# Where a diffusion block on one Trainium2 core waits for its earlier output stores: ahead of the issue of the last store, or behind it

## The chip, the cores and the metric

The kernel runs on one core of one Trainium2 chip. The metric is the device time of one execution in microseconds (us). One execution was also taken by the hardware profiler; its span runs from the first to the last profiled instruction, and positions such as "at 243.75" are microseconds from the start of that span. PE is the matmul engine, DVE the vector engine, ACT the scalar engine, POOL the GpSimd engine, and SP the engine that here does nothing but issue DMAs and wait on semaphores.

## What is computed

The reference is a transformer block with modulation, as diffusion models use it, for 2 batches of 256 tokens of width 1152, in bf16:

```python
mod = (silu(c) @ w_mod).reshape(B, 6, 1, D)
shift_a, scale_a, gate_a, shift_m, scale_m, gate_m = [mod[:, i] for i in range(6)]
h = layernorm(x) * (1 + scale_a) + shift_a
q, k, v = split(h @ wqkv)                 # 2 heads of 576
a = softmax(q @ k.T * Dh ** -0.5) @ v @ wo
x = x + gate_a * a
h2 = layernorm(x) * (1 + scale_m) + shift_m
m = gelu(h2 @ w_fc1) @ w_fc2              # 1152 -> 4608 -> 1152
return x + gate_m * m
```

Only the last line matters for the change: the product with `w_fc2`, the gate, the sum, and the store of the result.

## The kernel before, in words

**How the work is ordered.** The whole program is first written down as a list of small units, each for one engine, by helper functions (`dma` records its transfer at line 662, `mm` its matmul at line 681). `Sched.schedule` then plans them with estimated durations. For PE and SP the order is the order in which the units were written down; DVE and ACT take what is ready, the most urgent first. `Sched.emit` gives every instruction its waits and puts the instructions on the engines. A transfer that SP issues gets the next of 48 semaphores in turn, so the 14 output stores have one each, and no two of them share one. A DMA's semaphore is full, and the DMA "landed", when it has gone up by 16.

**The last stage** (lines 1131 to 1147). The 512 tokens are four tiles of 128 (`t`). Each tile's 1152 output columns are cut into pieces: three of 384 for tiles 0 to 2; 384, 384, 224, 96 and 64 for tile 3. A piece is 36 matmuls into one PSUM bank (line 1142), a DVE multiplication by the gate (line 1145), a DVE addition of the residual that writes the bf16 result (line 1146), and a store (line 1147, recorded at line 662) that SP issues when the addition is done. There are 14 pieces and so 14 stores, numbered here from 0: **store 11** is that of 224 columns (56 KB), **store 12** that of 96 columns (24 KB), **store 13**, the last, that of 64 columns (16 KB). In every one of them each of the 128 partitions writes one run of 448, 192 or 128 bytes for these three.

**The waits for stores.** The result buffers are three, used in turn, and DVE waits for the store that last used the buffer before it writes it again; those waits come from the planner and are not changed. Beside them SP itself waits for all stores, since the program must not end before they have landed. Where it does so is written by hand in `run_engine`, inside `emit`: `outs` is the list of the 14 stores in SP's order, `last_out` is store 13. Just ahead of `last_out` SP waits for `outs[:-2]`, stores 0 to 11 (lines 469 to 471), and then for the DVE addition of the last piece (line 476). Behind it SP waits for store 12 (lines 483 and 484) and for store 13 (line 485). In the program as it is built, SP has ahead of store 13 five instructions that each wait on two of the stores' semaphores (line 471), then one that waits on DVE and on store 1's semaphore (line 476); the wait for store 0 sits on the DMA instruction of store 13 itself. Behind it are one wait, for store 13 (line 485), and the branch that ends SP's part (line 554), which carries the wait for store 12. After it come SP's drain and the barrier of all engines.

Of the kernel before, what the change touches and what calls it, by code (L numbers as in the profile page):

```python
# [171 lines left out]
class Sched:  # L172
# [225 lines left out]
    def emit(self, nc, block, sems, dma_sems):  # L398
        order = self.order
        eidx = {e: 0 for e in ENGINES}  # L400
        dma_cnt = [0] * len(dma_sems)
        n_other = getattr(self, "n_other_dma_sems", 8)
        n_sp = len(dma_sems) - n_other
        di = 0
        dj = 0
        for e in ENGINES:
            for u in order[e]:
                for ins in u.instrs:
                    if u.dma_bytes > 0:
                        if e == "sp":  # L410
                            k = di % n_sp
                            di += 1
                        else:
                            k = n_sp + dj % n_other
                            dj += 1
                        dma_cnt[k] += 16
                        ins.dma_sem = k
                        ins.dma_val = dma_cnt[k]
                    else:
                        eidx[e] += 1  # L420
                        ins.eidx = eidx[e]
        self.final_counts = dict(eidx)
        self.final_dma = list(dma_cnt)
        snap = {}
        stats = {"waits": 0}

        def sem_of(d):
            if d.dma_sem is not None:
                return ("d", d.dma_sem), d.dma_val
            return ("e", d.unit.eng), d.eidx  # L430

        allu = sorted(self.units, key=lambda u: (u.start, u.uid))
        known = {e: {} for e in ENGINES}
        waits = {}
        for u in allu:
            e = u.eng
            kn = known[e]
            for ins in u.instrs:
                need = {}
                for d in ins.deps:  # L440
                    k, v = sem_of(d)
                    if need.get(k, 0) < v:
                        need[k] = v
                wl = []
                for k, v in sorted(need.items(), key=lambda kv: (-kv[1], str(kv[0]))):
                    if kn.get(k, 0) >= v:
                        continue
                    wl.append((k, v))
                    kn[k] = v
                    for d in ins.deps:  # L450
                        if sem_of(d) == (k, v):
                            sn = snap.get(d.gidx)
                            if sn:
                                for kk, vv in sn.items():
                                    if kn.get(kk, 0) < vv:
                                        kn[kk] = vv
                            break
                waits[ins.gidx] = wl
                stats["waits"] += len(wl)
                snap[ins.gidx] = dict(kn)  # L460
        self.wait_stats = stats

        outs = [ins for u in order["sp"] for ins in u.instrs if ins.is_out]
        last_out = outs[-1]

        def run_engine(e, eng_handle):
            for u in order[e]:
                for ins in u.instrs:
                    if ins is last_out:
                        for o in outs[:-2]:  # L470
                            eng_handle.wait_ge(dma_sems[o.dma_sem], o.dma_val)
                    for (k, v) in waits[ins.gidx]:
                        if k[0] == "d":
                            eng_handle.wait_ge(dma_sems[k[1]], v)
                        else:
                            eng_handle.wait_ge(sems[k[1]], v)
                    bi = ins.fn(eng_handle)
                    if ins.dma_sem is not None:
                        bi.then_inc(dma_sems[ins.dma_sem], 16)
                    else:  # L480
                        bi.then_inc(sems[e], 1)
            if e == "sp":
                for o in outs[-2:-1]:
                    eng_handle.wait_ge(dma_sems[o.dma_sem], o.dma_val)
                eng_handle.wait_ge(dma_sems[last_out.dma_sem], last_out.dma_val)

        block.sync(lambda eng: run_engine("sp", eng))
        block.tensor(lambda eng: run_engine("pe", eng))
        block.scalar(lambda eng: run_engine("act", eng))
        block.vector(lambda eng: run_engine("dve", eng))  # L490
        block.gpsimd(lambda eng: run_engine("pool", eng))
# [711 lines left out]
```

## Time and profile before

| | us |
|---|---|
| median of 3 runs | 248.95 (248.63 to 249.59) |
| the profiled execution's own time | 249.1 |
| its span, first to last instruction | 247.1 |
| PE busy in that span | 240.4 (97%) |
| mean granted clock of PE | 0.996 of full |
| last DVE instruction begins | 243.52 |
| store 13 is issued | 245.28 |
| last instruction begins | 247.08 |

The profiled execution's own time is 2.0 us more than its span, and 0.15 us above the median. The page has PE busy almost without a gap; its fifth part lists each group of instructions with the idle time of its engine before it, and its sixth the DMA issues with the median time from issue to landing. Beside the page, the trace answers for any stretch of time which instructions ran, what SP waited for, and how many DMA packets of each queue began in it. Queue q1 is the one on which SP's transfers run, 16 DMA engines in parallel; q8 and q14 carry instructions to the engines.

### The profile page before, as it was taken

To read this page: it belongs to the slowest core of one execution; us is meant where nothing else is said; L and a number is where in the kernel's file an instruction comes from. 1 tells how busy PE (TensorE), PEld (TensorE's weight loads), DVE (VectorE), ACT (ScalarE), POOL (GpSimd) and SP (SyncE) were. 2 spreads that over 40 slices of the span, in tenths; PEclk is the share of its full clock that TensorE was granted. 3 is DMA by queue.
4 is the path that set the end of the run, shared out by engine and by line. 5 is a ranking of instruction groups with operands and counts; after the bars stand their busy time and mean duration, and the time that the engine had idled before them with its cause. 6 is when DMAs were issued, how large, how long until landed. Compare 5 with 4: busy or idle time off the path is not lost.

```text
span 247.1 us, 4020 instructions
## 1 busy us (share of the span) xinstructions
PE 240.4 (97%) x1757; PEld 148.0 (60%) x1767; DVE 69.9 (28%) x179; ACT 64.0 (26%) x130; POOL 21.1 (9%) x35
## 2 busy tenths in 40 slices
PE   7999999999999999999999999999999999999993
PEld 2589844566656766798544444444666666666683
DVE  3742440546222779850000000000022111111122
ACT  5630340344312306983323332223000000000000
POOL 1300000000034175600000000000000000000000
PEclk9999999999999999999999999999999999999998
DMA  7999999999999999999953450000000000000000
GB/s 242 360 376 392 391 369 412 422 428 423 400 382 323 327 369 391 390 376 397 352 159 102 170 191 0 0 3 0 0 19 16 16 16 30 20 16 19 16 16 20
DMA packets 27708, 51.59 MB, mean 209 GB/s; under 512 B 1563, under 2 KB 15659, under 8 KB 26539
## 3 DMA queue, kind: packets, MB, share of 16 engines
q1 hardware_dynamic: 27216, 50.14, 56.1%
q0 software_dynamic: 448, 1.19, 1.5%
q8 instruction: 14, 0.23, 0.4%
q14 instruction: 3, 0.02, 0.0%
q10 hardware_dynamic: 27, 0.00, 0.0%
HBM read 50.14 MB, written 1.19 MB: 208 GB/s over the span
## 4 chain that ended last, share of the span: by engine, by line
PE 92%; DMA 3%; ACT 1%; SPq 1%; issue 0%; DVE 0%
PE psum L681 91%; DMA arena<-in_w_mod_dram 3%; PE psum L684 2%; ACT arena L1056 1%; SPq L662 1%; ACT arena L1040 1%; DVE arena L786 0%; DVE arena L1145 0%; DVE arena L1146 0%; DVE arena L777 0%
## 5 line engine op out<-in xcount | busy, mean ns | idle before, releaser
L681 PE MATMUL psum<-arena 128*128 128x384 bf16 (+8 forms) x1668 | 237.0, 312 | 2.4 <-POOL arena L704 1.4
L681 PEld LDWEIGHTS psum<-arena 128*128 128x128 bf16 (+1 forms) x1678 | 142.5, 97 | 92.2 <-issue 3.6
L1145 DVE TENSOR_TENSOR arena<-psum,arena 128x384 f32<-128x384 f32 (+3 forms) x14 | 7.0, 500 | 119.2 <-PE psum L681 119.2
L1066 ACT ACTIVATE arena<-psum 128x512 bf16<-128x512 f32 (+1 forms) x44 | 22.5, 522 | 42.6 <-PE psum L681 42.6
L676 ACT ACTIVATE arena<-psum 128x512 bf16<-128x512 f32 (+7 forms) x30 | 15.7, 546 | 35.7 <-PE psum L681 33.3
L678 DVE CAST arena<-psum 128x512 bf16<-128x512 f32 (+3 forms) x21 | 13.0, 627 | 26.4 <-PE psum L681 26.3
L1035 POOL TENSOR_TENSOR arena<-arena 128x384 f32<-128x384 f32 x12 | 10.9, 911 | 10.5 <-DVE arena L1034 9.3
L725 DVE BATCH_NORM_STATS2 arena<-arena 128x6 f32<-128x384 f32 (+1 forms) x18 | 9.5, 549 | 1.1 <-DMA arena<-in_x_dram 1.0
L1040 ACT ACTIVATE arena<-arena 128x1152 bf16<-128x1152 f32 x4 | 5.4, 1352 | 9.5 <-DVE arena L1039 9.5
L662 POOL DMA_DIRECT2D dit_scratch<-arena x4 | 2.7, 669 | 60.3 <-ACT arena L676 60.3
L684 PEld LDWEIGHTS psum<-arena 128*128 128x128 bf16 (+1 forms) x89 | 5.9, 98 | 2.7 <-DMA arena<-in_c_dram 0.8
L684 PE MATMUL psum<-arena 128*128 128x128 bf16 (+1 forms) x89 | 7.3, 219 | 0.2
L1034 DVE TENSOR_TENSOR arena<-psum,arena 128x384 f32<-128x384 f32 x12 | 6.6, 548 | 3.2 <-PE psum L681 2.6
L1146 DVE TENSOR_TENSOR arena<-arena 128x384 bf16<-128x384 f32 (+3 forms) x14 | 7.0, 501 | 0.5
L1056 ACT ACTIVATE arena<-psum,arena 128x128 bf16<-128x128 bf16 x16 | 6.1, 460 | 3.2 <-PE psum L684 2.5
L1053 DVE TENSOR_SCALAR arena<-psum,arena 128x128 bf16<-128x128 bf16 x20 | 5.5, 336 | 2.0 <-PE psum L684 1.8
L938 ACT ACTIVATE arena<-psum,arena 128x256 bf16<-128x256 f32 x8 | 3.7, 470 | 6.9 <-PE psum L681 5.4
L729 POOL TENSOR_TENSOR arena<-arena 128x1 f32<-128x1 f32 x6 | 3.3, 551 | 8.3 <-DVE arena L728 8.3
L901 ACT ACTIVATE arena<-arena 128x256 bf16<-128x256 bf16 x6 | 2.5, 495 | 3.3 <-DVE arena L895 3.3
L934 DVE TENSOR_REDUCE arena<-psum 128x2 f32<-128x512 f32 x4 | 2.8, 690 | 1.5 <-PE psum L681 1.5
L786 DVE TENSOR_SCALAR arena<-psum,arena 128x256 bf16<-128x256 bf16 x7 | 2.4, 349 | 2.7 <-PE psum L684 1.4
L942 DVE TENSOR_TENSOR arena<-arena 128x512 bf16<-128x512 bf16 x4 | 2.7, 687 | 0.1
(37 smaller groups left out, 32.0 us busy)
## 6 DMA issues: line engine op xcount, KB each, us to landing
arena<-in_w_mod_dram SPq DMA_DIRECT2D x3, 3456.0 KB, 26.5
arena<-in_w_fc_dram SPq DMA_DIRECT2D x9, 1152.0 KB, 8.8
arena<-in_w_fc_dram SPq DMA_DIRECT2D x4, 2592.0 KB, 20.9
arena<-in_wqkv_dram SPq DMA_DIRECT2D x18, 288.0 KB, 10.0
arena<-in_w_mod_dram SPq DMA_DIRECT2D x3, 864.0 KB, 12.5
arena<-in_wqkv_dram SPq DMA_DIRECT2D x1, 2592.0 KB, 10.9
arena<-in_wo_dram SPq DMA_DIRECT2D x1, 2592.0 KB, 39.0
arena<-in_w_mod_dram SPq DMA_DIRECT2D x3, 480.0 KB, 7.3
```

Source lines behind the costliest of these rows:

```text
L676: act(c_act(n), lambda e: e.activation(out=dst, in_=src, func=ACTF.Copy), [src], [dst], name)
L678: dve(c_dve_psum16(n) if psum16 else c_dve_psum32(n), lambda e: e.tensor_copy(dst, src), [src], [dst], name)
L681: S.instr(lambda e: e.matmul(o, lhsT=l, rhs=r, start=st, stop=sp, **kw), reads=[l, r], writes=[o])
L684: S.instr(lambda e: e.transpose(o, i_, idn), reads=[i_, idn], writes=[o])
L725: dve(550, lambda e, s=s, o=o: e.bn_stats(out=o, in_=s), [s], [o], "bn_%s_%d" % (tag, ci))
L1034: dve(550, lambda e, o=o, ga=ga, x1c=x1c: e.tensor_tensor(out=x1c, in0=o, in1=ga, op=ALU.mult), [o, ga], [x1c], "wo_t1_%d_%d" % (t, ci))
L1035: S.op("pool", 930, lambda e, xs=xs, x1c=x1c: e.tensor_tensor(out=x1c, in0=x1c, in1=xs, op=ALU.add), reads=[x1c, xs], writes=[x1c], name=" ...
L1040: act(1344, lambda e: e.activation(out=xn2, in_=x1, func=ACTF.Identity, scale=rs, bias=nm), [x1, rs, nm], [xn2], "xn2_%d" % t)
L1056: act(440, lambda e, o=o, dst=dst, s1=s1, s2=s2: e.activation(out=dst, in_=o, func=ACTF.Identity, scale=s1, bias=s2), [o, s1, s2], [dst], ...
L1066: act(c_act(ntok), lambda e: e.activation(out=dst, in_=o, func=ACTF.Gelu_apprx_tanh), [o], [dst], "gelu_%d_%d" % (f, tok0))
L1145: dve(c_dve_psum32(w), lambda e, o=o, gm=gm, t1=t1: e.tensor_tensor(out=t1, in0=o, in1=gm, op=ALU.mult), [o, gm], [t1], "fc2_t1_%d_%d" % ( ...
L1146: dve(c_dve_32(w), lambda e, t1=t1, x1c=x1c, ost=ost: e.tensor_tensor(out=ost, in0=t1, in1=x1c, op=ALU.add), [t1, x1c], [ost], "fc2_out_%d ...
```

## The change

SP no longer waits for stores 0 to 11 ahead of store 13. It issues store 13 as soon as the DVE addition of its piece is done, like every other store, and waits behind it for stores 0 to 12 and then for store 13.

```diff
             for u in order[e]:
                 for ins in u.instrs:
-                    if ins is last_out:
-                        for o in outs[:-2]:
-                            eng_handle.wait_ge(dma_sems[o.dma_sem], o.dma_val)
                     for (k, v) in waits[ins.gidx]:
...
             if e == "sp":
-                for o in outs[-2:-1]:
+                for o in outs[:-1]:
                     eng_handle.wait_ge(dma_sems[o.dma_sem], o.dma_val)
                 eng_handle.wait_ge(dma_sems[last_out.dma_sem], last_out.dma_val)
```

In the changed program as it is built, store 13's DMA instruction waits on DVE alone. Behind it stand seven wait instructions, the first on one semaphore and six on two (stores 7; 8 and 6; 9 and 5; 10 and 4; 11 and 3; 12 and 2; 13 and 1), and the closing branch carries the wait for store 0. SP has as many instructions as before, and the other engines have the same instructions in the same order. Three lines are gone from the file, so lines after 471 have numbers lower by three.

## The prediction

> **What bounds the kernel now.** I read the page first: its first part and its chain of waits.
>
> ```profile
> span 247.1 us, 4020 instructions
> PE 240.4 (97%) x1757; PEld 148.0 (60%) x1767; DVE 69.9 (28%) x179; ACT 64.0 (26%) x130; POOL 21.1 (9%) x35
> PE 92%; DMA 3%; ACT 1%; SPq 1%; issue 0%; DVE 0%
> ```
>
> PE sets the time up to its last matmul, and nothing that the diff touches is on PE. But that chain is followed back from the last DVE instruction, which ends at 243.75, and the span goes on to 247.1. The change can only act in these last 3.4 us, and there PE has nothing left to do. So I read that stretch by itself: its timeline, and then what SP waited for from 242 on (total, times, longest).
>
> ```profile
> 240.93 0.39 DVE L1146 TENSOR_TENSOR arena<-arena 128x224 bf16<-128x224 f32 x1
> 241.35 4.26 SPq L662 DMA_DIRECT2D out_dram<-arena  x3
> 242.32 0.26 DVE L1146 TENSOR_TENSOR arena<-arena 128x96 bf16<-128x96 f32 x1
> ...
> 243.52 0.23 DVE L1146 TENSOR_TENSOR arena<-arena 128x64 bf16<-128x64 f32 x1
> ```
>
> ```profile
> SPq L471 <- DMA out_dram<-arena: 1.9, 1, 1.9
> SPq L485 <- DMA out_dram<-arena: 1.1, 1, 1.1
> SPq L662 <- DVE arena L1146: 0.9, 1, 0.9
> ```
>
> The three last stores are issued from 241.35 on; the trace's records give 241.347, 242.610 and 245.279 for stores 11, 12 and 13. The last piece is done at 243.52 + 0.23 = 243.75, but its store goes out at 245.28: SP stands at line 471 for 1.9 us in one wait, and it is the fifth of the wait instructions there (from 243.2 to 245.15), the one that holds store 11. So the wait for a store of the piece before last is what holds the last store back.
>
> Why is store 11 late? The DMA view gives for any stretch the packets that began in it. First the issues with their times to landing (one row for stores 3 to 10, then 11, 12 and 13), then two stretches: 242.0 to 242.6 and 244.0 to 244.7.
>
> ```profile
> out_dram<-arena SPq DMA_DIRECT2D x8, 96.0 KB, 1.6
> ...
> out_dram<-arena SPq DMA_DIRECT2D x1, 56.0 KB, 3.8
> ...
> out_dram<-arena SPq DMA_DIRECT2D x1, 24.0 KB, 2.7
> ...
> out_dram<-arena SPq DMA_DIRECT2D x1, 16.0 KB, 1.4
> ```
>
> ```profile
> DMA packets 136, 0.07 MB, mean 117 GB/s; under 512 B 135, under 2 KB 135, under 8 KB 135
> ...
> q1 hardware_dynamic: 135, 0.05, 32.3%
> q8 instruction: 1, 0.02, 16.8%
> ```
>
> ```profile
> DMA packets 18, 0.01 MB, mean 7 GB/s; under 512 B 18, under 2 KB 18, under 8 KB 18
> ...
> q1 hardware_dynamic: 18, 0.01, 7.0%
> ```
>
> A store that meets nothing shows 144 packets on q1 (store 13 does, in 246.1 to 246.4): 128 rows and 16 small ones, nine on each of 16 DMA engines. Store 11 shows 135: one engine's nine are missing. In the same stretch one packet of 16 KB on q8, an instruction fetch, takes 16.8% of 16 engines over 0.6 us, which is 1.61 us of one engine, from 242.47 to 244.09. The missing nine, and nine of store 12, come right behind it: the 18 packets from 244.07 on. Store 11's semaphore has 15 of its 16 steps by 242.99 and the last at 245.14; store 12's by 244.10 and at 245.30. Store 8, issued at 226.53 and landed in 2.4 us instead of 1.6, met such a fetch too. So in this execution the waits ahead of store 13 do not pass for free: they wait for one DMA engine that is fetching instructions.
>
> **The change, part by part.**
>
> *The issue moves.* The two stores before it were issued 0.03 after their DVE addition (240.93 + 0.39 = 241.32 to 241.35; 242.32 + 0.26 = 242.58 to 242.61). Store 13 would go out at 243.75 + 0.03 = 243.78 instead of 245.28: **1.50 us earlier**. It issues one DMA and nothing else; no other queue is passed, since SP has nothing left to issue.
>
> *Its flight.* Store 13 took 245.279 to 246.693 = 1.41 us with no fetch beside it. From 243.78 the 15 free engines give 245.19. The engine that fetched is free at 244.09 and then has the 18 late packets until 244.67. Store 13's first packet began 0.83 after its issue, so at 243.78 + 0.83 = 244.61 in the changed kernel; its nine packets there come behind the 18. Two prices bound them. If they are as good as undisturbed, the store lands at 245.19 and store 12's 245.30 is the later. If the sixteenth engine's steps stay as far apart as those of stores 11 and 12 (245.14 to 245.30, 0.16), it lands at 245.30 + 0.16 = 245.46. Store 13's packets took 11 to 13 ns in this trace and store 12's on the late engine 20 to 49, so I take a point between, 245.40.
>
> [...]
>
> *The waits move behind.* Seven wait instructions and a branch now stand behind the issue, where one and a branch stood. SP's next instruction after issuing store 12 came 0.38 later (242.61 to 242.99), and waits that were already met followed each other every 0.06 to 0.07. So SP is at its first wait at 244.16 and past the fourth by 244.45, under the cover of the flight; without the cover the six added ones would cost 6 x 0.07 = 0.4. The fifth waits for store 11 until 245.15, the sixth for store 12 until 245.32, the seventh for store 13. If that has landed, SP is past it at 245.38, else 0.02 after the landing, at most 245.48. In the trace of before it is past this point at 246.71. The branch, the drain and the barrier behind it take 0.42 and stay: the branch then waits for store 0, landed long ago, as it now waits for store 12.
>
> *The sum.* 246.71 - 245.38 = 1.33 at best, 246.71 - 245.48 = 1.23 with the late engine; I take **1.25**. The span goes from 247.1 to 245.9, the profiled execution's 249.1 to 247.85. The median of the three runs is 0.15 below that execution, so the forecast is 248.95 - 1.25 = **247.7**.
>
> What is late next is store 11 itself, then 12, then 13, all on the engine that fetched: 0.1 us behind each other. The change takes the last store out of the queue behind the fetch, not the fetch out of the tail; the tail from 243.75 on would still hold 1.4 us of DMA and 0.4 of barrier.
>
> **The unknown.** The gain is as large as the stall, and the stall is as long as one fetch. The 14 fetches of 16 KB in the trace took 0.96 to 1.61 us, and the last is the longest. With 0.96 store 11 would land 0.65 earlier, at 244.48; store 13 of the kernel before would follow at 244.63 and land at 246.04, that of the changed kernel at 245.19 as before: gain 0.85. With no fetch in the way store 11 would have landed by 242.99, before the last piece is done, and only the wait instruction that carries DVE's semaphore goes, 0.07. A longer fetch raises both kernels and leaves 1.23. So the gain lies between 0.07 and 1.33.
>
> [...]
>
> **The rivals.**
> - *A shorter stall in the timed runs.* The profile is one execution, and its last fetch took 1.61 where the other 13 took 0.96 to 1.34. For it: that range. Against it: this fetch shares its engine with a store's packets at its start, and the profiled execution is only 0.15 slower than the median. Gain 0.85, **248.1**.
> - *No stall at all in the timed runs, or a landing that replaces it* (the last store takes its delay with it and lands after 246). Against it: most instructions that have to be fetched are PE's (3524 of the 4020), and those are the same in both. Gain under 0.1, **248.9**.
> - *Slower: the last store meets the fetch itself.* If the fetch began 1 to 2 us later in the changed kernel, store 13's share on that engine would be as late as store 11's was, 245.14 - 242.99 = 2.15 behind the other fifteen: 245.19 + 2.15 = 247.34 against 246.69, that is 0.65 slower, **249.6**. It decides from a fetch that ends after 245.6. Against it: PE reaches the same instruction at the same time, and no two of the trace's 16 KB fetches are closer than 9 us.
> - *That the change does not do what it says* can be left out: in the program as built, store 13 waits for DVE alone.
>
> **How the numbers follow.** Forecast 0.65, shorter stall 0.17, no stall 0.12, slower 0.06. The forecast's own range is 247.3 to 248.1 (1.23 to 1.33, and 0.3 for the median of a few runs, as the shown runs lie 0.3 below and 0.6 above theirs). The whole range takes in no stall, 248.9, and below 247.62 (1.33) the same scatter with some margin: 247.1 to 248.9. A change of 0.5%, about what a measurement of this kernel can tell from none, is 1.24 us; the forecast sits on that line. Of its 0.65 I put 0.48 beyond it; the rest, the shorter stall and no stall are within it. The slower case (0.65 us) is inside the line too, except with some scatter: 0.03.
>
> **What would show it.** Right: no wait at line 471's old place, store 13 issued at 243.8, 1.6 to 1.7 from issue to landing at most, store 11 still 3.8 and its wait now behind the issue, 18 or more late packets after the fetch, the span near 245.9. Wrong: a fetch in another place or of another length; store 13 needing over 2 us; or a tail of waits that goes on after the last landing by more than 0.1 above the present 0.42.

## The result, and the profile after

| | before | changed |
|---|---|---|
| median, first comparison | 249.0 us (6 runs, 248.1 to 249.59) | 247.55 us (6 runs, 247.18 to 248.06) |
| ratio, 95% interval | | 0.9947 [0.9924, 0.9971] |
| median, second comparison | 249.03 us (35 runs) | 248.01 us (12 runs) |
| ratio, 95% interval | | 0.9966 [0.9949, 0.9983] |
| span of the first profile | 247.1 us | 246.1 us |

The changed kernel is faster, by 1.45 us between the medians of the first comparison and by 1.02 in the second; the ratios, with their intervals, make it 0.7 to 1.9 us and 0.4 to 1.3. The forecast was 1.25 and a time of 247.7. These are the first two lines of the page of the changed kernel. PE has no more work than before: both programs have 1767 matmuls, of which the first trace lacks ten records.

```profile
span 246.1 us, 4030 instructions
PE 241.2 (98%) x1767; PEld 148.1 (60%) x1767; DVE 69.9 (28%) x179; ACT 64.0 (26%) x130; POOL 21.1 (9%) x35
```

Its timeline at the end, with line numbers lower by three than before:

```profile
241.54 3.02 SPq L659 DMA_DIRECT2D out_dram<-arena  x3
...
243.72 0.23 DVE L1143 TENSOR_TENSOR arena<-arena 128x64 bf16<-128x64 f32 x1
```

What SP waited for there (total, times, longest), and the three last stores from issue to landing:

```profile
SPq L659 <- DVE arena L1143: 4.5, 3, 2.8
SPq L481 <- DMA out_dram<-arena: 0.4, 1, 0.4
SPq L482 <- DMA out_dram<-arena: 0.2, 1, 0.2
```

```profile
out_dram<-arena SPq DMA_DIRECT2D x1, 56.0 KB, 3.7
out_dram<-arena SPq DMA_DIRECT2D x1, 24.0 KB, 2.6
out_dram<-arena SPq DMA_DIRECT2D x1, 16.0 KB, 1.7
```

The three issues now lie within 3.02 us instead of 4.26: store 13 follows its addition (243.72 + 0.23 = 243.94) at 243.97. SP's wait of 1.9 us for a store ahead of it is gone; 0.4 us of it is left behind the issue, at line 481. Store 11 is as late as before, 3.7 us. So what got faster is the moment at which the last store leaves.

The span holds a second thing that must be kept apart. The end of the last DVE addition came at 243.75 in the first profile of before and at 243.94 in that of the changed kernel; in a second profile of each, of the same programs, at 243.85 and 244.68. The part up to that addition thus differs by 0.1 us between the two executions of one program and by 0.7 between those of the other. All of this arises in the first 21 us: the second DVE instruction of line 777 (774 in the changed kernel, up to 779 in others) ends between 20.13 and 21.33 in the fourteen profiles of this study, and from there to the end of the last addition every one of them takes 223.36 to 223.41. I therefore read the **tail**, from the end of the last addition to the end of the span: 3.39 before, 2.16 changed. The difference, 1.23, is the change's gain in these two executions.

All kernels of this study, in us after the end of the last addition (negative: ahead of it), by the trace's records. The fetch is the last packet of 16 KB on q8. The last column is the median time of the timed runs; the kernel before had 248.79 to 249.03 in the comparisons in which these were taken.

| kernel | fetch ends | store 11 landed | store 13 issued | store 13 landed | tail | median |
|---|---|---|---|---|---|---|
| before | 0.34 | 1.39 | 1.53 | 2.95 | 3.39 | 249.0 |
| before, second profile | -0.01 | 1.05 | 1.19 | 2.60 | 3.04 | 248.76 |
| before, store 12 waited for ahead too | -0.31 | 0.67 | 0.98 | 2.39 | 2.78 | 248.82 |
| changed | 0.23 | 1.28 | 0.03 | 1.70 | 2.16 | 247.55 |
| changed, second profile | -0.39 | 0.64 | 0.03 | 1.44 | 1.90 | 248.01 |
| before, only stores 0 to 10 ahead | -0.09 | 1.00 | 0.09 | 1.51 | 1.96 | 248.06 |
| changed, last store on ACT | -0.39 | 0.66 | 0.03 | 1.50 | 1.95 | 247.94 |
| before, fetch moved away | -3.38 | -0.75 | 0.09 | 1.51 | 1.95 | 247.69 |
| changed, fetch moved away | -2.92 | -0.73 | 0.03 | 1.44 | 1.89 | 248.11 |
| before, 93 more matmuls | -10.33 | -0.71 | 0.10 | 1.51 | 1.95 | 248.17 |
| changed, 93 more matmuls | -10.39 | -0.76 | 0.03 | 1.44 | 1.89 | 247.89 |
| before, fetch on store 12 | 0.12 | -0.66 | 0.10 | 1.57 | 2.02 | 248.40 |
| changed, fetch on store 12 | 0.02 | -0.64 | 0.03 | 1.50 | 1.95 | 248.65 |
| changed, 120 more matmuls | -0.30 | -0.66 | 0.03 | 1.44 | 1.90 | 248.36 |

In the seven profiles in which store 11 was caught it lands 0.98 to 1.08 after the fetch ends, wherever that is. In the three of them whose kernel waits for it ahead of store 13, the tail is 2.78 to 3.39; in the four others it is 1.90 to 2.16.

### The profile page after: what moved, and what is told of

It reads as the page before. It is cut to its first block, busy times and chain, and to the rows that moved or that the text cites. A ratio compares the mean times of both kernels' runs of the same rounds, so it can differ in the third digit from the quotient of the medians.

```text
span 246.1 us, 4030 instructions
## 1 busy us (share of the span) xinstructions
PE 241.2 (98%) x1767; PEld 148.1 (60%) x1767; DVE 69.9 (28%) x179; ACT 64.0 (26%) x130; POOL 21.1 (9%) x35
## 3 DMA queue, kind: packets, MB, share of 16 engines
q0 software_dynamic: 448, 1.19, 1.4%
HBM read 50.14 MB, written 1.19 MB: 209 GB/s over the span
## 4 chain that ended last, share of the span: by engine, by line
PE 93%; DMA 3%; ACT 1%; SPq 1%; DVE 0%; issue 0%
PE psum L678 91%; DMA arena<-in_w_mod_dram 3%; PE psum L681 2%; ACT arena L1053 1%; SPq L659 1%; ACT arena L1037 1%; DVE arena L783 0%; DVE arena L1142 0%; DVE arena L1143 0%; DVE arena L774 0%
```

## The experiments

Theory A is the prediction's: the gain is what the last store lost by waiting for a store that sat behind an instruction fetch on one DMA engine. Theory B, the rival: the gain is the price of the wait instructions themselves, or of the step from a DMA's semaphore to SP, whatever fetches.

**The fetch moved away.** In the kernel before and in the changed one, PE gets 45 more matmuls at the very start, in the units that the program names `warm_b`, on data that nobody reads. If the count of PE's instructions decides where its next block of them is fetched, this moves the fetch; it did, from 1.27 us ahead of the end of the last addition to 4.51 and 3.86 ahead.

```diff
-                mm(ps32(2), IDENT, Q4B, True, True)
+                for j in range(4 if tag == "b" else 1):
+                    w = 128 if tag == "b" else 512
+                    mm(ps32(2, j * w, w), IDENT, Q4B[:, j * w:j * w + w], True, True)
```

> The kernel before, with 45 more matmuls in PE's warm-up at the very start (15 of 512 columns become 60 of 128, the same columns in all), so that PE's last instruction fetch comes some 45 matmuls earlier, 2 to 3 us, and is over before store 11's packets begin. Theory A, the change gains what store 11 loses behind that fetch: the last q8 packet begins near 239 to 240, store 11 lands in 1.6 to 1.7 us instead of 3.8, the wait ahead of store 13 is met before the last piece is done, store 13 is issued within 0.15 of the last DVE addition (it was 1.53 in the kernel before), and the kernel gains 1.4 us against before without the change. Theory B, the gain is the price of the six wait instructions and the step from a DMA's semaphore to SP, whatever fetches: store 13 still goes out 1.3 to 1.5 after the last addition, and the time stays within 0.3 us of before.

> The changed kernel with the same 45 more warm-up matmuls. Theory A: with the fetch out of the tail the change is worth only the wait instruction that goes, 0.07 us, so this and the kernel before with the fetch moved end within 0.15 of each other from the last DVE addition on; stores 11 to 13 land in 1.4 to 1.7 each. Theory B: it is still 1.2 faster than the kernel before with the fetch moved. On the longer issue of store 13 in the changed kernel (588 ns instead of 332, first packet 1.09 instead of 0.83 after the issue): if that was the third store standing behind a blocked DMA engine, the issue is back at 332 here; if two earlier stores in the queue are enough for it, it stays near 590.

The kernel before became as fast as the changed one (247.55 and 248.01 in its comparisons) without any change to its waits: 247.69 against 248.99 us, ratio 0.9954 [0.9937, 0.997]. SP's waits and the stores in it:

```profile
SPq L662 <- DVE arena L1148: 3.7, 2, 2.8
SPq L485 <- DMA out_dram<-arena: 1.1, 1, 1.1
SPq L476 <- DVE arena L1148: 0.5, 1, 0.5
```

```profile
out_dram<-arena SPq DMA_DIRECT2D x1, 56.0 KB, 1.6
out_dram<-arena SPq DMA_DIRECT2D x1, 24.0 KB, 1.5
out_dram<-arena SPq DMA_DIRECT2D x1, 16.0 KB, 1.4
```

Line 471 is no longer in the list: all waits for stores are met when SP comes to them, and what it waits for at line 476 is DVE. Store 11 lands in 1.6 us instead of 3.8. Beside it the changed kernel with the fetch moved has 248.11 us, ratio to before 0.9971 [0.9955, 0.9986]; its tail is shorter by 0.06, the one wait instruction. Between the medians of the pair the changed kernel is even 0.4 us the slower, but the two intervals overlap: with the stall gone the change is worth nothing that can be timed. Theory B falls here, since the wait instructions were all still there.

**Only store 11 taken from the waits ahead.**

```diff
-                        for o in outs[:-2]:
+                        for o in outs[:-3]:
...
-                for o in outs[-2:-1]:
+                for o in outs[-3:-1]:
```

> The kernel before, but ahead of store 13 SP waits for stores 0 to 10 only; the waits for 11 and 12 stand behind its issue. Eleven of the twelve waits stay where they were. Theory A, it is store 11 alone: as good as the changed kernel, 1.2 to 1.4 us under before, store 13 issued within 0.15 of the last DVE addition. Theory B, the waits cost by their number: a twelfth of the gain or one instruction in six, 0.1 to 0.2 us under before.

Measured 248.06 us, ratio 0.9959 [0.9943, 0.9976], and a tail of 1.96. The fetch still catches store 11; what SP waits for ahead of store 13, at line 476, is DVE:

```profile
SPq L476 <- DVE arena L1146: 0.5, 1, 0.5
```

```profile
out_dram<-arena SPq DMA_DIRECT2D x1, 56.0 KB, 3.4
```

Store 13 leaves 0.09 after the addition, against 0.03 in the changed kernel. So eleven of the twelve waits cost no more than these 0.06 where they were, and the rest of the loss was the wait for the one store. This run is the plainest proof of theory A: the fetch, the late store and eleven waits are all there, and the stall is not.

**One wait more ahead.** Store 12 is added to the list ahead of store 13.

```diff
-                        for o in outs[:-2]:
+                        for o in outs[:-1]:
...
-                for o in outs[-2:-1]:
-                    eng_handle.wait_ge(dma_sems[o.dma_sem], o.dma_val)
```

> The kernel before with one wait more ahead of store 13: store 12 too (stores 0 to 12 ahead, nothing but its own behind). Theory A: store 13 goes out 0.1 to 0.2 after store 12's last step, which is 0.16 after store 11's in the profile of before; so 0.1 to 0.3 us slower than before, 249.1 to 249.3, with a tail near 3.5 if the fetch ends where it did. Even with no fetch in the way store 12 would land only 1.45 after its issue, 0.33 after the last addition. Theory B: one wait more in an instruction that was there already, no difference.

The mechanism is as expected: store 13 went out at 0.98, which is 0.14 after store 12's last step at 0.83. The time is not: 248.82 us, ratio 1.0001 [0.9985, 1.0017], where 0.1 to 0.3 more was expected. In this execution the fetch ended 0.65 earlier than in the first profile of before, and the tail is 2.78. So an added 0.16 cannot be told from the fetch's own scatter.

**Both kernels once more, unchanged.**

> The changed kernel once more, unchanged, beside the others. Theory A: 1.0 to 1.4 us under before; tail from the last addition 2.0 to 2.2 according to where the fetch ends (in the first profile of it 0.23 after the addition), and the issue of store 13 longer than 332 ns only if the late packets of store 11 end more than 0.33 after that issue begins. Theory B makes the tail the same, 2.16, wherever the fetch ends.

> The kernel before once more, unchanged, for a second profile of it. Theory A with a stall of varying length: store 13's issue follows store 11's last step by 0.14, wherever that step falls (1.39 after the last addition in the first profile; 0.64 to 1.28 in the profiles of three other kernels with the fetch in the same place), so the tail is 2.6 to 3.4, and its excess over the 1.9 to 2.16 of the changed kernel is 0.7 to 1.2, which is where the gains of the timed runs, 1.0 and 1.45, should lie. If the first profile was the usual case, the tail is 3.2 to 3.5 again. Theory B: 3.39 whatever store 11 does.

The second profile of the changed kernel has a tail of 1.90, that of the kernel before 3.04. SP's wait in the latter and its store 11, 1.9 and 3.8 in the first profile:

```profile
SPq L471 <- DMA out_dram<-arena: 1.6, 1, 1.6
```

```profile
out_dram<-arena SPq DMA_DIRECT2D x1, 56.0 KB, 3.4
```

In both profiles of before, store 13 leaves 0.14 after store 11's last step (1.39 to 1.53, and 1.05 to 1.19) and the span ends 1.86 and 1.85 after it leaves. The stall is not a constant: it follows the end of the fetch, 0.34 after the addition in the one and 0.01 ahead of it in the other. From the two tails of each kernel the gain is anything from 3.04 - 2.16 = 0.88 to 3.39 - 1.90 = 1.49, and the two timed gains, 1.45 and 1.02, lie in that. The median of this repeat was 248.76 us, beside 248.79 of the same program in the same comparison.

**The fetch placed later.** More matmuls in the same place: 93, 110 and 120. In the first profile of before there are 249 records of matmuls and weight loads from one 16 KB fetch to the next on average; in that of the changed kernel, which lacks none, 251 (from 188 to 338 in single stretches), or 253 with the semaphore and drain records of PE's queue. So by an estimate from these, some 124 to 127 matmuls, each with its load, are one block; the expectations take 128, which no trace gives exactly.

```diff
-                mm(ps32(2), IDENT, Q4B, True, True)
+                for j in range({"b": 8, "e": 2, "c": 3}.get(tag, 1)):
+                    w = {1: 512, 2: 256, 3: 128, 4: 128, 8: 64, 9: 56}[{"b": 8, "e": 2, "c": 3}.get(tag, 1)]
+                    mm(ps32(2, j * w, w), IDENT, Q4B[:, j * w:j * w + w], True, True)
```

The diff is that with 110; with 93 the counts are b 7 and e 2 (pieces of 64 and 256 columns), with 120 they are b 8, e 4 and d 4.

> The kernel before with 93 more warm-up matmuls at the start (105 of 64 columns instead of 15 of 512, and 6 of 256 instead of 3), so that PE crosses an instruction block some 35 matmuls later than in the kernel before, within the last matmuls of all. The head of the program may get 1 to 3 us longer, so the tail is read from the last DVE addition on. Theory A: the fetch begins 0.6 to 1.1 before the end of the last addition, store 11's packets are through before it, store 11 lands in 1.7 us, the waits ahead of store 13 are met and it is issued within 0.15 of the addition; store 12, and store 13 if the fetch lasts past 0.86 after the addition, wait for the sixteenth engine instead; tail 2.0 to 2.7 instead of 3.39. Theory B (the price of the waits themselves): the issue still comes 1.3 to 1.5 after the addition.

> The changed kernel with the same 93 more warm-up matmuls. Theory A: no gain is left, the tail from the last addition on is that of the kernel before with the late fetch within 0.3 us, since both now wait for stores 12 and 13 behind the fetch. Theory B: 1.2 faster than it. On the long issue: only store 12 can stand unread at the blocked engine when store 13 is issued. If the issue is held while two earlier stores stand there, it takes 332 ns here; if one is enough, it takes 500 or more.

The placement missed: with 93 more matmuls the last fetch of all ended 10 us ahead of the last addition, and none came in the tail. The pair repeats the first one: 248.17 and 247.89 us, ratios 0.9972 [0.9955, 0.9989] and 0.9958 [0.994, 0.9976], tails 1.95 and 1.89, and the change is worth 0.06 in the tail.

> The kernel before with 110 more warm-up matmuls (120 of 64 columns for 15 of 512, 6 of 256 for 3, 3 of 128 for 1). With 93 more the last fetch had gone from the tail altogether, 10 us before the last addition; 110 are 18 fewer than the 128 that bring PE to the same place of the next instruction block, so if that block is fetched at all, it is fetched some 18 matmuls of 64 columns, 0.5 us, later than in the kernel before. Theory A, if it is: store 11 gets through (1.7 us), the waits ahead of store 13 are met, store 12 is the late one (2.2 to 3.0 us), and the tail from the last addition on is 1.95 to 2.4. If it is not fetched, tail 1.95. Theory B: tail 3.2 to 3.5 in both cases.

> The changed kernel with the same 110 more warm-up matmuls. Theory A: no gain beside the kernel before with them, 0.06 us for the one wait instruction, whether the fetch comes and catches store 12 (tail 1.9 to 2.4) or does not come (1.9). Theory B: 1.2 under it.

With 110 the fetch came 0.4 us later than in the kernel before (it begins 0.84 ahead of the end of the last addition, there 1.27; at 29 ns from one matmul of 64 columns to the next in the first profile of before, that is some 15 matmuls, where 18 were expected) and caught store 12 instead of 11. The stores in the kernel before with it, and SP's waits in the changed kernel with it:

```profile
out_dram<-arena SPq DMA_DIRECT2D x1, 56.0 KB, 1.7
out_dram<-arena SPq DMA_DIRECT2D x1, 24.0 KB, 2.3
out_dram<-arena SPq DMA_DIRECT2D x1, 16.0 KB, 1.5
```

```profile
SPq L481 <- DMA out_dram<-arena: 0.4, 1, 0.4
SPq L482 <- DMA out_dram<-arena: 0.3, 1, 0.3
```

Now the fetch is in the tail, but on a store that the kernel before does not wait for ahead of the last issue, and the two kernels are alike: 248.40 and 248.65 us, ratios to before 0.9997 [0.9982, 1.0013] and 0.9992 [0.998, 1.0005], tails 2.02 and 1.95. These tails are nearly as short as the fetch-free ones, and yet the ratios show no gain over before, and the medians lie only 0.4 and 0.2 below the 248.83 of before. By the profiles, only the first 21 us differ beyond the tail, as shown above. The DVE instruction of line 777 named there ends at 20.89 and 21.06 in these two profiles, 20.37 and 20.44 in those of before; but kernels with the short warm-up have anything from 20.16 to 21.33, so what the longer warm-up costs at the head is not shown.

> The changed kernel with 120 more warm-up matmuls (120 of 64 for 15 of 512, 12 of 128 for 3 of 512, 8 of 128 for 2 of 512), 8 fewer than a whole block: if the block is fetched, 0.2 us later than in the changed kernel. If store 11 is caught and its late packets end more than 0.36 after the last addition, the issue of store 13 lasts until they end (over 332 ns, as the 588 in the first profile of the changed kernel), and store 13's first packet comes that much later; if they end sooner, or if store 11 is not caught, it is 332. If the issue is longer while store 11's packets are through, the queue was not what held it.

Store 11 was through before this fetch, which caught store 12 alone (landed 2.0 us after its issue). Store 13's issue took 332 ns. So what was to be learned about the long issue was not. It was 248.36 us, ratio 0.9977 [0.9962, 0.9993].

**The last store on another queue.**

```diff
-        outs = [ins for u in order["sp"] for ins in u.instrs if ins.is_out]
+        outs = [ins for e in ("sp", "act") for u in order[e] for ins in u.instrs if ins.is_out]
...
-                dma(outv[b, :, t % 2, c0:c1], ost, P * w * 2, "st_out_%d_%d" % (t, c0), is_out=True)
+                dma(outv[b, :, t % 2, c0:c1], ost, P * w * 2, "st_out_%d_%d" % (t, c0), is_out=True,
+                    eng="act" if (t, c1) == (3, D) else "sp")
```

> The changed kernel, but the last store is issued by ACT, idle since 172, on its own DMA queue; SP waits behind its own stores as in the changed kernel. If the 588 ns of the last issue is SP's queue being full behind the blocked engine, the issue on ACT is not held, its first packet comes 0.8 to 0.9 after the issue, and the store lands about 0.25 us earlier than in the changed kernel (1.4 after the issue instead of 1.68); then store 12, at 1.45 after the last addition, ends the program, and the tail from the last addition on is 1.9 to 2.0 instead of 2.16. If the issue is slow for another reason, or the sixteenth DMA engine is late for ACT's queue too, the tail stays at 2.1 to 2.2 and the time within 0.1 us of the changed kernel.

It gains nothing over the changed kernel: 247.94 us, ratio 0.9962 [0.9947, 0.9977], tail 1.95. As a test it is inconclusive. In its profile store 11's late packets were over before store 13 was issued, so the case to be tested, an issue with those packets still due, did not occur. ACT's issue took 382 ns against SP's 332, and the store 1.47 us against 1.41.

No version is clearly below the changed kernel: without the two longest warm-ups, the medians of all that take the last issue out of the stall lie between 247.55 and 248.17.

## Why the prediction was right, step by step

- *The issue moves.* Right to the hundredth: 0.03 after the addition in all profiles of the changed kernel, against 1.53 and 1.19 before.
- *The flight.* The size was right, 1.68 us where 1.41 to 1.68 was given and 1.62 taken, but for another reason, so that it came out is luck. I had the last store late on its sixteenth DMA engine. In the first profile of the changed kernel its sixteen steps came together, from 1.53 to 1.70; the whole store was late, since its issue took 588 ns instead of 332 and its first packet came 1.09 after it instead of 0.83. In the second profile there is nothing of this, and the flight is 1.41.
- *What is late next.* Right in the first profile: stores 11, 12 and 13 landed at 1.28, 1.45 and 1.70. In the second, with 0.64 and 0.81, the last store's own flight set the end, and the floor under the tail is 1.41 of flight, 0.03 of issue and 0.45 of waits, branch and barrier.
- *The waits behind.* Right: met waits followed each other every 0.06 to 0.07, all under the flight, and the end of the span came 0.45 after the last landing, 0.44 before.
- *The sum.* 1.25 was forecast from the first profile of before, and its tail is 1.23 longer than that of the first profile of the changed kernel. That the two agree so closely is luck in part: the fetch happened to end late in both, 0.34 and 0.23 after the addition. Between the second profiles it is 3.04 - 1.90 = 1.14. The span came out 0.2 longer than the 245.9 forecast, because the part ahead of the last addition was 0.2 longer in that execution.
- *The unknown.* This was the weak step. The prediction took the stall of one profiled execution, whose fetch of 1.61 us was the longest of all, as the likeliest, and let only the length of the fetch vary. Its start moves too, from 1.42 to 0.94 ahead of the end of the addition in the seven profiles with the fetch on store 11. In the ten profiles with a fetch in the tail its packet took 0.88 to 1.61, and store 11, in the seven where it was caught, landed at 0.64 to 1.39. The rival with a shorter stall, 0.85 us, and the forecast are two points of one scatter; the timed runs, with 1.02 and 1.45, do not tell them apart. The 1.45 is above the 1.33 that the prediction gave as the most, and the interval of that comparison, 0.7 to 1.9, reaches below it.
- *No stall in the timed runs.* False as far as the runs show: store 11 is late in all seven profiles of kernels with the short warm-up, and taking the stall away from the kernel before gained 0.93 us where the wait for store 11 went behind and 1.30 and 0.86 where the fetch was moved by 45 and 93 matmuls. Moved by 110 it gained nothing that the ratio shows, as said above.
- *Slower, by the last store meeting the fetch.* Not reached. The latest fetch that I could place caught store 12 and ended 0.12 after the last addition. One that falls on store 13 itself was not had, so its price stays an estimate.
- *What the fetch costs, and the order of landing.* With the fetch on a store that is waited for, the tail of the kernel before is 3.39 and 3.04 us, with the fetch moved away 1.95. Stores 11, 12 and 13 landed in this order in both profiles of the changed kernel, but no run shows the landing of store 13 held up by that of store 12 on one DMA engine, as the forecast's 245.40 had it, 0.10 behind store 12's 245.30: its flight is 1.41 to 1.47 in thirteen of the fourteen profiles, and in the other, with 1.68, its sixteen steps came together.

## What to carry to other kernels

A wait that is "long met" by the plan is only free if it is met in every execution: put waits that merely close the program behind the last issue, where the last transfer's own flight covers them (here 1.41 us or more, against 0.06 to 0.07 for each wait that is met). Read the tail from the end of the last computation, not the span, and look on the instruction queues for what a late DMA engine was doing. And before a stall in one profile is taken as the gain, a second profile of the same kernel is worth having: here the stall was 1.50 in one and 1.16 in the other.

## What the runs showed of the hardware that was not expected

- **One DMA engine seems to be taken before the fetch's packet begins.** The profile does not name the engine of a packet; that one is late shows in store 11's semaphore, with 15 of its 16 steps in time, and in the late packets, which in the seven profiles begin as the fetch ends. In the first profile of the changed kernel store 11's packets began 1.57 ahead of the end of the last addition and the fetch's packet 0.94 ahead, yet nine of the store's 144 packets are missing ahead of the fetch too. Two stretches of that trace, 242.0 to 242.75 and 244.1 to 244.8, show 135 packets and then 18:

```profile
q1 hardware_dynamic: 135, 0.05, 25.8%
...
q1 hardware_dynamic: 18, 0.01, 7.0%
```

  The first stretch has no packet of q8 at all. What holds the engine from there on was not found.
- **The issue of a store can take longer.** 588 ns in the first profile of the changed kernel, ending at 0.62 like store 11's late packets; 400 and 388 in the two kernels with 110 more matmuls, whose fetch is on store 12; 332 or 333 in all other cases on SP, that with 120 more matmuls and its fetch on store 12 among them. The supposition of the expectations, a queue that holds an issue while two earlier stores stand unread at one engine, fits the first and not the 400 and 388, for which store 11 was through. No trace shows what a queue holds, and the cause stays open.
- **The instruction count decides.** The fetch that costs over a microsecond sits in the tail only because of how many instructions PE has: 45 matmuls more, whose results nobody reads, took it out of the tail (3.39 and 3.04 us became 1.95) and gained as much as the change did.
